# Retention and two feed-forward layers: heads loaded whole, VectorE and GpSimd work of retention in a written order, weight conversions spaced anew

## The chip, the cores and the metric

The kernel runs on one core of a Trainium2 chip. Time is device microseconds (us) from start to end of one execution. Engine names below: TensorE (PE, matrix products; PEld, its loads of weights), VectorE (DVE), ScalarE (ACT), GpSimd (POOL), SyncE (SP, which issues the DMA transfers).

## The reference

Four batches of eight heads, 576 positions of 64 dimensions, go through retention; its output, 2304 rows of 512, goes through two feed-forward layers. Cut to what matters:

```python
scores = (1 / sqrt(64)) * q @ k.T                     # each head, 576 x 576
Dmat   = where(i >= j, gamma[head] ** (i - j), 0)     # decay with distance
ret    = (scores * Dmat) @ v                          # 4 x 8 x 576 x 64
x      = ret.transpose(0, 2, 1, 3).reshape(2304, 512)
h      = ((x @ w1) * (x @ w2)) @ w3                   # 2304 x 1024
x      = h @ w_out                                    # 2304 x 512
h      = x @ w_in                                     # 2304 x 2048
g      = maximum(h, 0) + alpha * minimum(h, 0)
out    = g @ w_out2                                   # 2304 x 512
```

Inputs and output are float32 in the reference; the weights arrive as 64-bit values and are turned into pairs of a rounded high part and a low part on the chip.

## The kernel before

**Stages.** Retention runs from 0 to 126 us. The stage from 126 to 308 us makes (x @ w1) * (x @ w2) in 24 groups (3 parts of x by 8 units of weights), each by seven block products where the plain way takes eight. From 308 to 352 us w3 @ w_out is folded into one matrix, while x still waits; 352 to 452 us multiplies by it. From 452 to 642 us comes x @ w_in with the activation ("stage G" below, groups GGroup), and then g @ w_out2 to the end.

**Retention.** Heads go in pairs, two heads on the two halves of 64 partitions; a batch has four pairs. The sequence is cut into five chunks (four of 128 and one of 64). For one chunk TensorE makes the scores of its positions among themselves (`scores`, L391), VectorE multiplies them by a mask (L395, or L383 for the short chunk); TensorE makes the moments k v of the chunk (`moments`, L406), VectorE adds them to the state aged so far (L412 for the first chunk, L414), GpSimd ages the new state by the decay of a chunk (L418); TensorE makes the values (`values`, L433 from the state, L442 from the masked scores), and ScalarE copies them into x (`parts`, L454). Ahead of that GpSimd scales q by position (`scale`, L368 for 512 columns, L370 for 64), and ScalarE scales k (`prep`, L361). Batch 0 is done in two parts of two pairs (`r0`, `r1`, six steps each); batches 1 to 3 are a chain of fifteen links of four pairs: link i makes the scores of chunk i + 1, the values of chunk i and the moments of chunk i + 1. The PSUM tile of the moments is one, that of the scores is double. The table `beside` says what else stands behind which link: scales of the next batch (`ready`), loads, conversions of the first weights, and operands made of x (`x_steps`).

**Halves.** In x, the two heads of an odd pair stand in the other order than in memory. Before, odd pairs (and their constants) are loaded with their two halves exchanged: `in_places` splits a load into two of 64 rows.

**Buffers of heads.** Batches 0 and 2 share one room (heads_r), 1 and 3 another (heads_l, the last pair elsewhere). So batch 2 loads once batch 0 has been read, and batch 3 once batch 1 has.

**Weights.** A piece of 128 x 512 weights is loaded (raw) and goes through four steps: ScalarE `_first` (L92, L93), VectorE `_second` (L102 to L107, four passes), ScalarE `_third` (the high part), VectorE `_fourth` (the low part, L121). Units of w1 and w2 (`AbUnits`) are two pieces, with VectorE sums of their quarters (`sums`, L564 to L567) and low halves of these (L557). Operands of x are differences (L630), rounded by ScalarE (L622), with low halves on VectorE (L626). Eight pairs of pieces of w_out2 (`ops2`) are converted where there is room: three in the stage from 126 us, five in stage G; each has a multiplication by the sign of alpha (L294), differences (L277) and high and low halves (L245, L254); in the earlier stage VectorE does differences and signs together (L275), in stage G GpSimd does. In stage G the raw pieces (`rawo`) and the results on their way to memory share three buffers.

**Order.** TensorE, ScalarE and SyncE run in the order in which the code is written. VectorE and GpSimd are ordered by a scheduler, by its own estimate of when operands are ready; each engine then runs its row in order. `spot` and `at` place work between products: a group has three positions, a, b and c, and "5b" is position b of group 5. In stage G ScalarE also copies a product bank for the next group's sums (L1260), which TensorE (L779) waits for.

## Time and profile before

| | us |
|---|---|
| median of three runs | 827.45 (825.82 to 829.76) |
| the profiled execution | 826.97 |
| its span on the core | 825.2 |
| TensorE busy | 760.3 (92%) |
| VectorE busy | 627.7 (76%) |
| ScalarE busy | 423.5 (51%) |
| GpSimd busy | 66.8 (8%) |

The stages above are cuts of the span by the first and last products of each. The mean granted clock of TensorE over the span is 0.959 of full speed. In a timeline, the bracket behind an instruction tells how long its engine stood idle ahead of it, and what ended that; SPq is SyncE's issue of a transfer, not the transfer.

### The profile page before, as it was taken

How to read it: one execution, taken by the hardware profiler on the slowest of the kernel's cores; microseconds unless marked ns; L12 is line 12 of the kernel's file. 1: busy time of each engine (PE TensorE's matmuls, PEld its weight loads, DVE VectorE, ACT ScalarE, POOL GpSimd, SP SyncE). 2: the span in 40 equal slices, each digit the busy share in tenths (PEclk: the TensorE clock that was granted, in tenths of full speed). 3: DMA queues.
4: the chain of work that ended last, by engine and by line, in shares of the span. 5: the costliest groups of instructions: out<-in, count | busy, mean ns of one | idle time of the engine just before them, and what ended most of it. 6: DMA issues, size and time to landing. Idle time of an engine off the chain costs nothing.

```text
span 825.2 us, 13389 instructions
## 1 busy us (share of the span) xinstructions
PE 760.3 (92%) x4977; PEld 707.5 (86%) x4979; DVE 627.7 (76%) x1028; ACT 423.5 (51%) x750; POOL 66.8 (8%) x81
## 2 busy tenths in 40 slices
PE   6657579999999999999999969989999999999998
PEld 3546469999999998899999969989999888888887
DVE  1115897899989896998998756877877688887784
ACT  1214446566656654676765635645654454444443
POOL 1422510000000000000000302122020000000000
PEclk8759898999999999999999988999999999999999
DMA  6973801467755798659673888767599954444440
GB/s 159 301 218 105 260 27 36 158 202 243 255 194 175 264 341 320 203 182 401 207 282 120 266 303 282 254 237 250 158 316 378 316 163 127 129 127 128 134 147 26
DMA packets 103249, 173.26 MB, mean 210 GB/s; under 512 B 9872, under 2 KB 68496, under 8 KB 103184
## 3 DMA queue, kind: packets, MB, share of 16 engines
q1 hardware_dynamic: 103184, 172.41, 62.7%
q8 instruction: 39, 0.64, 0.3%
q14 instruction: 26, 0.21, 0.1%
HBM read 112.34 MB, written 60.03 MB: 209 GB/s over the span
## 4 chain that ended last, share of the span: by engine, by line
PE 75%; DMA 12%; DVE 5%; issue 2%; SPq 2%; ACT 2%; POOL 1%; ACTq 0%; DVEq 0%; POOLq 0%
PE h L779 35%; PE o L1369 13%; PE y L1187 12%; PE o L1371 7%; PE pw L1027 5%; DMA heads_r<-in_qk_dram 2%; DMA heads_l<-in_qk_dram 2%; DMA heads_r<-in_kv_dram 2%; DMA cells<-gd 2%; DMA xs<-in_qk_dram 1%; DMA gd<-g 1%; PE o L442 1%; DMA wod<-wo2u 1%; DMA pair<-in_qk_dram 1%; SPq L475 1%
## 5 line engine op out<-in xcount | busy, mean ns | idle before, releaser
L1187 PE MATMUL y<-yab,wa 128*128 128x384 f32 x576 | 100.0, 334 | 0.0
L1187 PEld LDWEIGHTS y<-yab,wa 128*128 128x128 f32 x576 | 99.9, 188 | 0.1
L1350 DVE TENSOR_TENSOR cells<-cells,cells 128x1024 fp32r<-128x1024 f32 x63 | 76.3, 1220 | 26.4 <-ACT cells L1344 26.3
L1369 PE MATMUL o<-wa,cells 128*128 128x512 f32 x288 | 76.6, 393 | 0.0
L1344 ACT CAST cells<-cells 128x1024 fp32r<-128x1024 f32 x63 | 64.9, 1052 | 7.5 <-DVE cells L1337 4.5
L779 PE MATMUL h<-xT,wa 128*128 128x384 f32 x288 | 57.7, 342 | 10.5 <-ACT h L1260 10.5
L779 PEld LDWEIGHTS h<-xT,wa 128*128 128x128 f32 x288 | 51.6, 192 | 11.8 <-ACT h L1260 11.4
L1369 PEld LDWEIGHTS o<-wa,cells 128*128 128x128 f32 x288 | 51.4, 189 | 8.5
L1369 PE MATMUL o<-wop,cells 128*128 128x512 f32 x216 | 57.0, 392 | 0.8 <-DVE cells L1381 0.8
L779 PE MATMUL h<-xB,wa 128*128 128x384 f32 x288 | 57.5, 338 | 0.0
L779 PE MATMUL h<-xl,wa 128*128 128x384 f32 x288 | 54.9, 336 | 1.2 <-ACT h L802 1.2
L779 PE MATMUL h<-wa 128*128 128x384 f32 x264 | 51.1, 342 | 1.3 <-ACT h L802 1.3
L779 PEld LDWEIGHTS h<-xl,wa 128*128 128x128 f32 x288 | 50.1, 188 | 2.4 <-ACT h L802 2.1
L779 PEld LDWEIGHTS h<-xB,wa 128*128 128x128 f32 x288 | 51.4, 191 | 0.0
L779 PEld LDWEIGHTS h<-wa 128*128 128x128 f32 x264 | 47.6, 193 | 1.9 <-ACT h L802 1.9
L294 POOL TENSOR_TENSOR a<-a,al 128x512 f32<-128x512 f32 x10 | 11.0, 1100 | 462.8 <-DVE a L107 462.8
L1369 PEld LDWEIGHTS o<-wop,cells 128*128 128x128 f32 x216 | 39.4, 188 | 8.7 <-issue 1.0
L779 PE MATMUL h<-xr,wa 128*128 128x384 f32 x240 | 45.6, 335 | 1.4 <-DVE xs L818 1.4
L454 ACT COPY xs<-o 128x256 f32<-128x256 f32 (+2 forms) x27 | 11.8, 444 | 68.0 <-PE o L442 62.4
L1371 PEld LDWEIGHTS o<-wa,cells 128*128 128x128 f32 x288 | 41.8, 190 | 3.5
L1371 PE MATMUL o<-wa,cells 128*128 128x256 f32 x288 | 44.5, 282 | 0.0
L1242 DVE SCALAR_TENSOR_TENSOR g<-h,al,g 128x384 f32<-128x384 f32 x48 | 29.4, 612 | 18.9 <-ACT g L1241 17.6
(233 smaller groups left out, 1621.6 us busy)
## 6 DMA issues: line engine op xcount, KB each, us to landing
gd<-g SPq DMA_DIRECT2D x96, 192.0 KB, 4.3
cells<-gd SPq DMA_DIRECT2D x36, 512.0 KB, 5.9
abd<-xs SPq DMA_DIRECT2D x24, 384.0 KB, 2.8
yf<-abd SPq DMA_DIRECT2D x24, 384.0 KB, 6.1
rawi<-in_w_in_dram SPq DMA_DIRECT2D x16, 512.0 KB, 5.9
raw<-in_w_dram SPq DMA_DIRECT2D x14, 512.0 KB, 4.3
wod<-wo2u SPq DMA_DIRECT2D x28, 256.0 KB, 4.5
wa<-wod SPq DMA_DIRECT2D x12, 512.0 KB, 5.7
```

The source lines that it names most:

```text
L294: nc.gpsimd.tensor_tensor(out=a, in0=a, in1=sg[:, i:i + 1].to_broadcast([P, 512]), op=ALU.mult)
L442: nc.tensor.matmul(o[pp, p % 2, m // 2, 0:w], vj, rj, start=(c == 0 and m < 2), stop=True, skip_group_check=True)
L454: nc.scalar.copy(dst, o[:, :, :, lo:up].rearrange("p r i w -> p i r w"))
L475: nc.sync.dma_start(out=t[rows], in_=src[pp])
L779: nc.tensor.matmul(ps, a[:, x, ks], b[:, y, k], start=(fresh and n == 0), stop=(n == 5), skip_group_check=True)
L1027: nc.tensor.matmul(acc[i], a[:, ic], bb, start=(k == 0 and n == 0), stop=(k == C1 - 1 and n == 2))
L1187: nc.tensor.matmul(ys[o], wpc[c][a][:, oc], yab[u][:, bb, c % 2], start=(c == 0 and i == 0), stop=(c == C1 - 1 and i == 2))
L1242: nc.vector.scalar_tensor_tensor(out=g, in0=ps, scalar=sal[:, c], in1=g, op0=ALU.mult, op1=ALU.max)
L1344: nc.scalar.copy(h.bitcast(F32R), self.q[name])
L1350: nc.vector.tensor_tensor(out=l.bitcast(F32R), in0=q[name], in1=h, op=ALU.subtract)
L1369: nc.tensor.matmul(ps, h[:, k], w[k], start=(fresh and k == 0), stop=(k == C1 - 1), skip_group_check=True)
L1371: nc.tensor.matmul(ps[:, 256:], l[:, k], w[k][:, 0:256], start=False, stop=(k == C1 - 1), skip_group_check=True)
```

## The change

Heads and constants are loaded whole: `in_places` goes, every pair takes a q, k load and a k, v load of 128 rows, constants of two pairs come in one load. `places` now gives the rows as loaded, and the other half for an odd pair's output, so values are written to the exchanged half. Pieces of w1 and w2 have the row halves of their odd blocks exchanged to match (`Turned`): three loads each. In retention VectorE and GpSimd run in the written order too (`ordered`). Ages of batch 0 go to VectorE, the others stay on GpSimd; scales of four of the sixteen pairs go to VectorE. The first two units of weights are converted earlier. GpSimd takes: the differences of x, the sums of all units but the first, the low parts of 24 pieces of w3 and w_out (`Pieces._fourth`), and all sums and signs of ops2, four pairs of which (three before) are made ahead of stage G. The steps of these conversions are spaced anew (WS, OPS0, OPS1, `spots`), and in stage G each pair of ops2 takes ten steps instead of seven, with the loads of the next one last. Some VectorE additions from PSUM get a higher priority with the scheduler (`soon`). Pieces of the fold lie at other places (`pieces_at`) and are fetched a little earlier.

The diff, cut to its core:

```diff
@@ -342,8 +335,7 @@
     def places(p):
-        x = p % 2
-        return [(HEADS[(j + x) % 2], HEADS[j], (j + x) % 2) for j in range(2)]
+        return [(HEADS[j], HEADS[(j + p) % 2], j) for j in range(2)]
@@ -353,21 +345,22 @@
+            self.age = nc.gpsimd if b else nc.vector
@@ -493,22 +472,17 @@
-        if p % 2:
-            in_places(p, x, qk[b, p])
-            nc.sync.dma_start(out=y[:, 0:16], in_=kv[b, p, :, 0:16])
-            in_places(p, y[:, 16], kv[b, p, :, 16])
-        else:
-            nc.sync.dma_start(out=x, in_=qk[b, p])
-            nc.sync.dma_start(out=y, in_=kv[b, p])
+        nc.sync.dma_start(out=x, in_=qk[b, p])
+        nc.sync.dma_start(out=y, in_=kv[b, p])
@@ -524,19 +498,30 @@
+    class Turned(Weights):
+        def load_until(self, n):
+            while self.loaded < min(n, len(self.pieces)):
+                i = self.loaded
+                t = self.raw[i] = self.raw_room(i)
+                dst, src = (x.rearrange("p (k n) -> p k n", k=KT) for x in (t, self.pieces[i][0]))
+                nc.sync.dma_start(out=dst[:, 0::2], in_=src[:, 0::2])
+                for a, b in (HEADS, HEADS[::-1]):
+                    nc.sync.dma_start(out=dst[a, 1::2], in_=src[b, 1::2])
+                self.loaded += 1
@@ -558,13 +543,14 @@
         def sums(self, c):
...
+            engine = nc.vector if c == 0 else nc.gpsimd
@@ -648,7 +634,7 @@
-        return x_operands(p, place, in_sums)
+        return x_operands(p, place, in_sums, nc.gpsimd)
@@ -660,28 +646,36 @@
-    nc.sync.dma_start(out=kd, in_=c_row[:, 0:H])
-    load_constants(0)
-    load_constants(1)
+    nc.sync.dma_start(out=al_row, in_=c_row)
+    load_constants(0, 1)
     load_pair(0, 0)
     load_pair(0, 1)
-    load_ages()
-    load_constants(2)
-    load_constants(3)
+    load_constants(2, 3)
...
+    ordered = ExitStack()
+    ordered.enter_context(tc.manual_schedule(engines={mybir.EngineType.DVE, mybir.EngineType.Pool}))
@@ -733,19 +722,22 @@
     beside = {
-        3: [lambda: make.extend(ab_operands(0)), x_steps(1), ready(rs[2], 0, 1, 2, 3), ab_steps(0, "s0")],
...
+        3: [ready(rs[2], 2), ready(rs[2], 3, nc.vector), x_steps(1)],
...
-        8: [ready(rs[3], 0, 1, 2, 3), ab_steps(0, "l0")],
...
+        8: [ready(rs[3], 1), ready(rs[3], 2), ready(rs[3], 3, nc.vector), ab_steps(1, "l0")],
@@ -840,34 +836,44 @@
-    PRE, PAIRS_IN_X = 10, 3
+    PRE, PAIRS_IN_X = 10, 4
...
+        def _fourth(self, i):
+            hi, lo = self.dest.pop(i)
+            nc.gpsimd.tensor_tensor(out=lo, in0=self.ab.pop(i)[0], in1=_f32(hi), op=ALU.subtract)
@@ -1423,11 +1433,13 @@
-        ops2.add(m, 7 * (m - PAIRS_IN_X), ("fx", "sx gx fy", "sy gy h1", "l1 t1 h2", "l2 t3 h3", "l3 h4 x", "l4 y"), m + 1 < C1)
+        ops2.add(m, 10 * (m - PAIRS_IN_X), ("fx", "sx gx fy", "sy gy", "h1 t1", "l1 h2 t3", "l2 h3", "l3 h4", "l4", "x", "y"),
+                 m + 1 < C1)
@@ -1448,12 +1460,9 @@
-    for at_spot in (4, 13, 27, 35):
...
+    spots = ("2a 2b 2c 3a 3b 3c 4a 4b 5a 5b", "8c 9a 9b 9c 10a 10b 10c 11a 11b 11c",
+             "12c 13a 13b 13c 14a 14b 14c 15a 15b 15c", "17c 18a 18c 19a 19c 20a 20b 20c")
```

What the order of the engines' rows becomes, in three places. In these rows a name is that of the room in which an operand lies (heads_r and heads_l are the rooms of the heads, al the constants), and a line is that of its own kernel.

SyncE where batch 1's first pairs are loaded, before (qk is q and k, kv is k and v):

```order
L510 DMA heads_l_98<-in_qk_dram 128x1152
L511 DMA heads_l_98<-in_kv_dram 128x1088
L475 DMA heads_l_98<-in_qk_dram 64x1152 x2
L507 DMA heads_l_98<-in_kv_dram 128x1024
L475 DMA heads_l_98<-in_kv_dram 64x64 x2
```

and after, with the first piece of w1 and w2 (raw0):

```order
L485 DMA heads_r_102<-in_kv_dram 128x1088
L484 DMA heads_l_98<-in_qk_dram 128x1152
L485 DMA heads_l_98<-in_kv_dram 128x1088
L509 DMA raw0_129<-in_w12_dram 128x2x128
L511 DMA raw0_129<-in_w12_dram 64x2x128 x2
```

The odd pair's five transfers are two like the even pair's, and a weight piece has three.

GpSimd around the first links of the chain, before (L368 and L370 are scales, L418 ages; the 128 wide ones are of batch 0):

```order
L370 TENSOR_TENSOR heads_l_98<-heads_l_98 128x64
L418 TENSOR_TENSOR heads_l_98<-heads_l_98,al_72 128x128
L368 TENSOR_TENSOR xs_94<-xs_94,heads_l_98 128x512
L370 TENSOR_TENSOR xs_94<-xs_94,heads_l_98 128x64
L418 TENSOR_TENSOR heads_l_98<-heads_l_98,al_72 128x128
L368 TENSOR_TENSOR heads_r_102<-heads_r_102,heads_l_98 128x512
```

and after (L361 and L363 are scales, L411 ages; the last scale here is of batch 2):

```order
L361 TENSOR_TENSOR xs_94<-xs_94,heads_l_98 128x512
L363 TENSOR_TENSOR xs_94<-xs_94,heads_l_98 128x64
L411 TENSOR_TENSOR heads_l_98<-heads_l_98,al_72 128x256 x2
L361 TENSOR_TENSOR heads_r_102<-heads_r_102,heads_l_98 128x512
L363 TENSOR_TENSOR heads_r_102<-heads_r_102,heads_l_98 128x64
```

No age of batch 0 stands in the row any more, and batch 1's ages come behind all its scales.

ScalarE in stage G, before (h are product banks, a and b the first step of a piece, rawo the raw piece, wo2u the results):

```order
L245 CAST wo2u4_3_4640<-t3_3_4614 128x2x256
L1255 ACTIVATE u23_4660<-h3_1_4620,al_72 128x384
L1241 ACTIVATE g3_4668<-h3_0_4619,al_72 128x384
L1241 ACTIVATE g2_4683<-h2_1_4528,al_72 128x384
L1260 COPY h4_1_4702<-h4_0_4701 128x384
L1255 ACTIVATE p54_4717<-h4_2_4703,al_72 128x384
L1255 ACTIVATE u24_4735<-h4_1_4702,al_72 128x384
L1241 ACTIVATE g4_4743<-h4_0_4701,al_72 128x384
L92 ACTIVATE a8_4747<-rawo8_4642 128x512
L93 ACTIVATE b8_4748<-rawo8_4642 128x512
L1241 ACTIVATE g3_4757<-h3_1_4620,al_72 128x384
L92 ACTIVATE a9_4780<-rawo9_4675 128x512
```

and after (L251 is the old L245, L94 the old L92):

```order
L1265 ACTIVATE p52_4563<-h2_2_4549,al_72 128x384
L94 ACTIVATE a8_4565<-rawo8_4423 128x512
L95 ACTIVATE b8_4566<-rawo8_4423 128x512
L1265 ACTIVATE u22_4585<-h2_1_4548,al_72 128x384
L1249 ACTIVATE g2_4593<-h2_0_4547,al_72 128x384
L94 ACTIVATE a9_4602<-rawo9_4425 128x512
L95 ACTIVATE b9_4603<-rawo9_4425 128x512
L1249 ACTIVATE g1_4612<-h1_1_4476,al_72 128x384
L1270 COPY h3_1_4636<-h3_0_4635 128x384
```

Piece 8 stood in group 4, behind the results of pair 3; it now stands in group 2, and pair 3 is no longer made in this stage.

## Rows read from the trace of the kernel before

**Rows 1.** Stretches of the program, busy us by engine, clock and DMA.

```profile
core 0: us, PE busy (x) PEld busy (x) DVE busy (x) ACT busy (x) POOL busy (x), PEclk, DMA share, GB/s
0.00:126.00 126.00, 82.37 (x1182) 63.52 (x1185) 62.25 (x98) 41.43 (x85) 37.31 (x51) 0.78 0.61 178
20.00:50.00 30.00, 20.34 (x245) 15.49 (x245) 6.26 (x14) 6.19 (x16) 10.74 (x16) 0.67 1.02 299
126.00:308.00 182.00, 178.04 (x1009) 175.75 (x1008) 158.88 (x319) 112.28 (x221) 0.00 (x0) 0.99 0.61 207
452.00:642.00 190.00, 177.01 (x997) 174.49 (x996) 140.04 (x231) 98.76 (x183) 29.53 (x30) 0.97 0.80 271
```

**Rows 2.** PE's waits in retention, 0 to 126 us: total, times, longest.

```profile
PE st L406 <- DVE heads_l L414: 14.6, 4, 4.8
```

**Rows 3.** Timeline, 53 to 58 us: start, us, instruction, idle before and releaser.

```profile
54.83 1.26 POOL L368 TENSOR_TENSOR heads_r<-heads_r,heads_l 128x512 f32<-128x512 f32 x1 [2.81 <-DMA heads_r<-in_qk_dram]
56.32 0.40 POOL L418 TENSOR_TENSOR heads_l<-heads_l,al 128x128 f32<-128x128 f32 x1
56.76 0.29 DVE L414 TENSOR_TENSOR heads_l<-heads_l,st 128x128 f32<-128x128 f32 x1 [8.29 <-POOL heads_l L418]
57.19 0.49 PE L433 MATMUL o<-heads_r,heads_l 64*64 64x64 f32 x8 [6.47 <-DVE heads_l L414]
57.73 0.33 SPq L510 DMA_DIRECT2D heads_r<-in_qk_dram  x1
```

**Rows 4.** Loads by tile: count, KB each, median us from issue to landing.

```profile
heads_r<-in_qk_dram SPq DMA_DIRECT2D x4, 576.0 KB, 4.3
heads_r<-in_kv_dram SPq DMA_DIRECT2D x4, 544.0 KB, 6.2
```

**Rows 5.** Timeline of the start: first load of heads, first full scores.

```profile
5.15 0.58 SPq L510 DMA_DIRECT2D heads_r<-in_qk_dram  x1
16.59 0.80 PE L391 MATMUL sc<-heads_r 64*128 64x128 f32 x4 [5.00 <-POOL heads_r L368]
```

**Rows 6.** Timeline, TensorE in the last batch: first scores of two links.

```profile
107.68 0.94 PE L391 MATMUL sc<-heads_l 64*128 64x128 f32 x12
113.59 0.94 PE L391 MATMUL sc<-heads_l 64*128 64x128 f32 x12
```

**Rows 7.** Instructions by line: busy us, mean ns of one, idle before.

```profile
L626 DVE TENSOR_TENSOR xr<-xs,xr 128x768 fp32r<-128x768 f32 x6 | 5.7, 951 | 4.9 <-ACT xr L622 4.9
L121 DVE TENSOR_TENSOR xs<-xs 128x512 fp32r<-128x512 f32 x10 | 6.8, 681 | 0.0
L565 DVE TENSOR_TENSOR xs<-xs,a 128x256 f32<-128x256 f32 x6 | 2.5, 414 | 0.0
L102 DVE TENSOR_SCALAR a<-a 128x512 f32<-128x512 f32 x15 | 6.2, 417 | 0.0
L294 POOL TENSOR_TENSOR a<-a,al 128x512 f32<-128x512 f32 x10 | 11.0, 1100 | 462.8 <-DVE a L107 462.8
L277 POOL TENSOR_TENSOR t<-a,t 128x256 f32<-128x256 f32 x10 | 8.4, 844 | 0.4
```

**Rows 8.** Timeline, GpSimd and VectorE at once, in two places.

```profile
90.34 1.35 POOL L368 TENSOR_TENSOR heads_l<-heads_l 128x512 f32<-128x512 f32 x1 [2.51 <-DMA heads_l<-in_qk_dram]
90.48 1.49 DVE L102 TENSOR_SCALAR a<-a 128x512 f32<-128x512 f32 x1
69.53 1.22 DVE L395 TENSOR_TENSOR heads_l<-sc,heads_l 128x1024 f32<-128x1024 f32 x1
69.69 0.61 POOL L418 TENSOR_TENSOR heads_l<-heads_l,al 128x256 f32<-128x256 f32 x1 [0.54 <-DVE heads_l L414]
```

**Rows 9.** Timeline of stage G, where TensorE stands longest.

```profile
490.10 0.66 ACT L92 ACTIVATE a<-rawo 128x512 f32<-128x512 f32 x1 [6.31 <-DMA rawo<-in_w_out_dram]
496.25 2.29 PE L779 MATMUL h<-xT,wa 128*128 128x384 f32 x6 [7.88 <-ACT h L1260]
```

**Rows 10.** TensorE's waits in stage G, 452 to 642 us.

```profile
PE h L779 <- ACT h L1260: 12.4, 5, 7.9
```

More of the change, by code (lines that the diff above doesn't have):

```diff
@@ L355, in __init__, with prep @@
             self.rt, self.state = {}, {}
-        def prep(self, pairs=None):
-            for p in pairs or self.pairs:
+            self.age = nc.gpsimd if b else nc.vector
+        def prep(self, pairs):
+            for p in pairs:
                 k = kvt[self.b][p]
@@ L470, in retention_moe_kernel, with load_constants @@
     qt, kt, kvt, vt = ({b: {} for b in range(B)} for _ in range(4))
-    def in_places(p, t, src):
-        for rows, pp, _ in places(p):
-            nc.sync.dma_start(out=t[rows], in_=src[pp])
-    def load_constants(p):
-        if p % 2 == 0:
-            nc.sync.dma_start(out=per_pair[:, p], in_=c_pair[:, p])
-            return
-        in_places(p, qs[:, p], c_pair[:, p, 2 * CH + 64:])
-        for h in range(2):
-            nc.sync.dma_start(out=mask[:, h, p], in_=c_pair[:, p, (1 - h) * CH:(2 - h) * CH])
-        in_places(p, mtail[:, p], c_pair[:, p, 2 * CH:2 * CH + 64])
-    def load_ages():
-        nc.sync.dma_start(out=gc[:, 0::2], in_=c_row[:, H::2])
-        in_places(1, gc[:, 1::2], c_row[:, H + 1::2])
+    def load_constants(*pairs):
+        ps = slice(pairs[0], pairs[-1] + 1)
+        nc.sync.dma_start(out=per_pair[:, ps], in_=c_pair[:, ps])
     def load_pair(b, p):
@@ L680, in retention_moe_kernel, with ready, run @@
     busy(26)
+    rs = [None] + [Retention(b, list(range(NPAIR)), psum0) for b in range(1, B)]
     r0, r1 = Retention(0, [0, 1], psum0), Retention(0, [2, 3], psum0)
     s0, s1 = r0.steps(), r1.steps()
-    r0.scale()
-    r0.prep()
+    def ready(r, p, engine=nc.gpsimd):
+        def run():
+            r.scale([p], engine)
+            r.prep([p])
+        return run
     def keep_busy(step):
@@ L691, in keep_busy @@
         return run
-    def ready(r, *ps):
-        def run():
-            r.scale(ps)
-            r.prep(ps)
-        return run
-    rs = [None] + [Retention(b, list(range(NPAIR)), psum0) for b in range(1, B)]
     chain = [(b, c) for b in range(1, B) for c in range(NCH)]
@@ L712, in link, with ab_steps @@
         return run
+    def ab_steps(c, steps):
+        return lambda: abu.run(c, steps)
     b = keep_busy
-    for step in (b(s0[0]), b(s0[1]), b(s0[2]), b(s0[3]), ready(r1, 2), s0[4], ready(r1, 3), s1[0],
-                 s0[5], s1[1], s1[2], ready(rs[1], 0), s1[3], ready(rs[1], 1), s1[4], ready(rs[1], 2), s1[5],
-                 ready(rs[1], 3)):
+    for p in range(2):
+        ready(r0, p, nc.vector)()
+    for step in (b(s0[0]), b(s0[1]), b(s0[2]), ready(r1, 2), b(s0[3]), ready(r1, 3), s0[4], s1[0], s0[5], s1[1],
+                 ab_steps(0, "f0"), s1[2], ready(rs[1], 0), ab_steps(0, "s0"), s1[3], ready(rs[1], 1), ab_steps(0, "h0 f1"),
+                 s1[4], ready(rs[1], 2), ab_steps(0, "s1 l0"), s1[5], ready(rs[1], 3), ab_steps(0, "h1")):
         step()
@@ L720, in retention_moe_kernel @@
     load_batch(2)
-    abu.load(2)
+    abu.load(4)
     def x_steps(n):
         return lambda: some_of(make, n)
-    def ab_steps(c, steps):
-        return lambda: abu.run(c, steps)
     def to_xr():
@@ L826, in p3 @@
             u = self.f[:, 1]
-            nc.vector.tensor_tensor(out=u, in0=self.b3, in1=u, op=ALU.add)
-            nc.vector.tensor_tensor(out=u, in0=u, in1=self.p5s, op=ALU.mult)
+            with soon():
+                nc.vector.tensor_tensor(out=u, in0=self.b3, in1=u, op=ALU.add)
+                nc.vector.tensor_tensor(out=u, in0=u, in1=self.p5s, op=ALU.mult)
             later.append(self.spill)
@@ L1247, in from_sum @@
             g = self.tile("g", 8)
[L1248 to L1249 removed]
+            with soon():
+                nc.vector.scalar_tensor_tensor(out=g, in0=a, scalar=sg[:, c], in1=b, op0=ALU.mult, op1=ALU.add)
+                nc.vector.scalar_tensor_tensor(out=g, in0=g, scalar=al[:, c], in1=g, op0=ALU.mult, op1=ALU.max)
             keep(2 * self.j + m, 2 * self.p + t, g)
```

204 lines of the change are left out of this document (104 added, 100 removed).

## The prediction

> **What bounds the kernel now.** I read the stretches first, then the waits of TensorE in the stretches where it stands, then the timeline around the longest waits. In the two big product stages TensorE is the bound: from 126 to 308 us it is busy 178.04 of 182.00 us at a clock of 0.99 of full speed, and from 452 to 642 us 177.01 of 190.00 [rows 1]. Retention is another thing. In its 126 us TensorE is busy 82.37, at a clock of 0.78, VectorE 62.25, and the DMA engines 0.61 of the time [rows 1]; nothing is full on the average. From 20 to 50 us the DMA share is 1.02 at 299 GB/s, so there the loads are the bound; later they are not.
>
> The waits say who is late: TensorE's moments L406 wait 14.6 us in four times for VectorE's state addition L414 [rows 2]. The timeline of one more such wait, of the values L433, says why [rows 3]. At 54.83 GpSimd runs a scale L368 after standing 2.81 us for a load; only then does the age L418, queued behind it, run (56.32); VectorE adds at 56.76 after 8.29 idle; TensorE goes on at 57.19 after 6.47; and the next load of a heads' buffer, which needs TensorE's last reads, is issued at 57.73. That is a circle: the load holds GpSimd, GpSimd the state, the state the values, and these the next load. It comes with each batch.
>
> **Retention, part by part.** Removed: the half-row loads and the many constant loads. All pairs now come in two full-height DMAs of 576 and 544 KB, constants in two of 448 KB, and the odd pairs' swap of halves is done where TensorE writes the values, at no instruction. Loads taken as one stream at 299 GB/s [rows 1] plus 2.5 us (taken between nothing and the whole 4.3 or 6.2 us to landing [rows 4], most of which the stream itself hides), and from 1.3 us instead of 5.15 [rows 5], since two issues stand ahead of the first, not eight (5.15 x 2 / 8): pair (0,1) is there after 2.75 MB at 13, where before the first full scores stood at 16.59 after 5.00 us of waiting [rows 5]; batch 1's last pair after 11.1 MB (the other constants and two w12 pieces lie between) at 41; batch 2 after 15.7 MB at 56.
>
> A link (scores, values, moments of one chunk of four pairs) takes (113.59 - 107.68) / 2 = 2.95 us on TensorE where nothing stands [rows 6]. Batch 0's twelve steps have half a link's heads each, so between 1.5 and 2.95; with the middle, 27 us, they end at 39 to 40. So batch 1 starts with its last load at 41.5. Sixteen links would then end at 88.7. They don't quite: batch 3's buffers are those of batch 1, whose last values are read at about 59 (five links from 41.5 give 56.3, and these values stand behind ScalarE's scaling of pair (2,3), which now comes ahead of the copy of o1_3). From 59, 4.59 MB take 15.3 + 2.5 us, so 77; the scale of (3,3), now on VectorE, makes it 78.6, where TensorE would have been ready at 71. Six links of 3.0 to 3.2 follow: 97, the last copies 1.5 more, and the product stage starts at **98.5** for 126 now, the cut of [rows 1]. **Gain 27.5.** The bounds: 91.5 if batch 3's load costs nothing (88.7, 1.3 for the longer last links, 1.5 for the copies), 108.5 if VectorE is the bound (below).
>
> That rests on the ages not being late again. Ages of batch 0 go to VectorE (six of 128x128, at 0.29 each by its addition of that size [rows 3], 1.7 us, in stretches bound by loads); those of the others stay on GpSimd, after all scales of batch 1, and only three scales of each later batch stand among them. A scale of batch 2 can still stand for its load, with an age behind it and TensorE behind that; by the sums above its loads are there at 56 and wanted from 50 to 57, so one wait of up to 3 us is possible and lies inside the 77. VectorE, now in written order, has two such places too, the scales of (2,3) and (3,3), with the tail mask L383 and the next masks L395 behind them and TensorE's values behind these. The w12 pieces take three DMAs of 1 KB rows instead of one each (48 issues for 16); at 0.33 us an issue [rows 3] that is 32 x 0.33 = 10.6 us of SP's time spread over two stages; each is issued a place ahead, so I cost it nothing. If that lead is gone a place costs one landing, 4 to 6 us [rows 4].
>
> VectorE's own work from 41.5 on: 12 masks x 1.22 [rows 8] = 14.6; 13 low halves L626 x 0.951 = 12.4; five low halves of weights and eight conversion passes near 0.681 = 8.9; 15 small ones x 0.413 = 6.2 [rows 7]; two scales near 0.8 each: 44, ending at 85.5. GpSimd's: 9 ages x 0.61 and 6 scales x 1.35 [rows 8] with tails of 0.3; 7 differences of x, 768 wide, at 1.5 x 1.100 and 4 sums x 0.844 [rows 7]: about 31. Side by side both fit under TensorE.
>
> **The stage at 126 to 308.** VectorE loses 24 sums x 0.413, 10 low halves x 0.681 [rows 7] and four differences, and gets a fourth pair of w_out2: 158.88 [rows 1] becomes about 140. GpSimd, at nothing before, gets 40 sums x 0.844, 18 operations x 1.100 [rows 7] and 6 differences x 1.65: 63. TensorE idles only 182.00 - 178.04 = 3.96 there, so no more can come. The earlier place of its additions saves perhaps 2 of these; GpSimd beside VectorE gives them back. **0**, between -3 (a gain) and +21 (below).
>
> What the two do to each other the trace shows in rows: at 90.34 GpSimd's scale and at 90.48 VectorE's pass L102 run together, and L102 takes 1.49 us [rows 8] for 0.417 elsewhere [rows 7]; at 69.53 a mask, whose one source is PSUM, takes its 1.22 beside an age of 0.61, and neither is stretched [rows 8]. [...]
>
> In the fold, 14 low halves go from VectorE to GpSimd: 14 x 0.681 = 9.5 less there, 14 x 1.100 = 15.4 more here [rows 7]; I cost it at nothing, since VectorE is relieved by what GpSimd, idle until then, takes, and at up to 4 if the last piece is late by a few of these. The stages y and out aren't touched.
>
> **Stage 452 to 642.** TensorE idles 190.00 - 177.01 = 12.99 [rows 1], 12.4 of it before L779 for ScalarE's copy L1260, in five waits, the longest 7.9 [rows 10]. The chain: ScalarE stands 6.31 us at 490.10 for a load of rawo, with L1260 behind it, and TensorE begins at 496.25 after 7.88 [rows 9]. Raw pieces and results share three buffers, and the load was asked for one position after the result whose buffer it takes. Now loads stand last of ten steps, three positions after it, and four ahead of their use (a position is 190 / 72 = 2.6 us, so 10.5 against a landing of 4 to 6 [rows 4]); one pair fewer is done here, and the first has its load ahead of the stage. I leave 2.4 of the 12.4 and add 1 for the lower clock after a long stop (0.97 here, 0.99 above [rows 1]): **gain 11**, between 0 and 13.
>
> **Sum.** 825.2 - 27.5 - 0 - 11 = 786.7, and with the 1.8 us that the profiled execution has around its span 788.5: **789**. That execution (826.97) lies 0.5 under the median of the three runs, which changes nothing.
>
> **The rivals.** (a) VectorE becomes the bound of retention: if half of GpSimd's 31 us holds it up, 44 + 15.5 at nine tenths busy is 66 from 41.5, so the stage starts at 108.5: 799. For it: the stretched L102, and a written order that lets nothing pass. Against: masks are free of it, and TensorE waits at the loads anyway. (b) The stop at rawo only moves to another pair: gain 0 there, 800. For it: pair 6 still has its load right behind stores of results on SP. Both: 811. (c) Slower: GpSimd and VectorE take turns throughout. In the stage of 182 us that is 140 + 63 = 203, so 21 more; it decides once what can't overlap adds to more than 182. In retention 44 + 31 at 0.87 from 41.5 gives 128, so 2 more: 827 + 21 + 2 - 11 = 839. For it: L102 at 90.48 [rows 8]. Against: a mask from PSUM lies beside GpSimd untouched [rows 8]; the stage has 72 additions from PSUM of 384 columns, about 0.55 each between 0.413 and 0.681 [rows 7], 39 us, and without these the turns add to 164. (d) Loads come faster than 299 GB/s, batch 3 isn't waited for, the stage starts at 91.5: 782. [...]
>
> **How the numbers follow.** The forecast (780 to 796) has 0.53; (a) 0.17, (b) 0.12, both 0.03, (c) 0.06, (d) 0.09. The range takes all but (c) and the ends: **774 to 813**. It goes below (d) by the 2 us of the second stage and all 13 of the fourth. 0.5% (4 us) is about what a measurement can tell from no change: over that faster 0.91, within 0.03, slower 0.06.
>
> **What would show it.** Right: first AB product at 95 to 102; loads without a gap until batch 1 is in, then one gap until about 59; no age waiting behind a scale for over 3 us; TensorE busy 178 in a stage of 181 to 184; at most 4 us of waits for L1260. Wrong: VectorE busy over nine tenths from 42 to 98 with TensorE waiting for its masks or low halves (a); ScalarE again standing 5 us for rawo (b); the second stage over 190 with L102 and its like at 1 us (c).

## The result and the profile after

The changed kernel takes 809.12 us, median of 4 runs (807.9 to 809.31), beside 827.78 before: a ratio of 0.9771, 95% interval 0.9746 to 0.9797. It is faster, as forecast, and inside the range of 774 to 813, but by 18.7 us where 38.5 were forecast. Half of the gain is missing: the groups of w1 and w2 lost 16.0 of the 38.3 us that retention and stage G won.

Stages of the two profiled executions, from the start of the first product of one stage to that of the next (us):

| stage | before | after | change | forecast |
|---|---|---|---|---|
| retention | 125.5 | 102.2 | -23.3 | -27.5 |
| groups of w1 and w2 | 182.9 | 198.9 | +16.0 | 0 |
| fold | 43.5 | 46.3 | +2.8 | 0 |
| y | 99.9 | 100.1 | +0.2 | 0 |
| stage G | 190.1 | 175.1 | -15.0 | -11 |
| out, to the end of the span | 183.3 | 183.5 | +0.2 | 0 |
| span | 825.2 | 806.1 | -19.1 | -38.5 |

The stretches of the changed kernel in the columns of [rows 1] (length, then busy us of TensorE, its weight loads, VectorE, ScalarE and GpSimd, the clock, the DMA share and GB/s):

```profile
0.00:102.00 102.00, 73.89 (x1174) 58.13 (x1178) 70.16 (x102) 42.18 (x87) 46.88 (x48) 0.88 0.58 214
102.00:301.00 199.00, 182.82 (x1034) 177.93 (x1024) 174.87 (x279) 115.10 (x229) 76.25 (x66) 0.98 0.62 214
...
447.00:622.00 175.00, 173.63 (x997) 172.38 (x996) 133.88 (x218) 96.40 (x176) 24.28 (x24) 1.00 0.81 278
```

In the second row VectorE is busy 174.87 us where the forecast had 140, and GpSimd 76.25 where it had 63; TensorE idles 16 us, against 4 in the same row of [rows 1]. In the third TensorE idles 1.4, against 13.

What TensorE waits for in the second stage, before (total, times, longest):

```profile
PE h L779 <- ACT h L802: 2.6, 2, 1.3
PE h L779 <- DVE xs L818: 1.4, 1, 1.4
```

and after (L812 is the old L818, an addition of VectorE; L795 the old L802, ScalarE's copy of a product bank):

```profile
PE h L772 <- DVE xs L812: 9.5, 8, 3.0
PE h L772 <- ACT h L795: 5.7, 4, 2.3
```

The instructions of VectorE in that stage tell more (line, engine, operation, shapes and count, then busy us, mean ns, idle before):

```profile
L824 DVE TENSOR_TENSOR xs<-xs 128x384 f32<-128x384 f32 x23 | 18.7, 813 | 0.1
...
L817 DVE TENSOR_TENSOR xs<-h,xs 128x384 f32<-128x384 f32 x24 | 13.3, 553 | 11.3 <-PE h L772 11.1
L812 DVE TENSOR_TENSOR xs<-h,xs 128x384 f32<-128x384 f32 x24 | 13.2, 550 | 3.7 <-PE h L772 3.7
...
L612 DVE TENSOR_TENSOR xl<-xs,xl 128x768 fp32r<-128x768 f32 x8 | 11.2, 1406 | 0.7 <-ACT xl L608 0.7
L104 DVE TENSOR_SCALAR xs<-xs 128x512 f32<-128x512 f32 x18 | 10.6, 587 | 2.7 <-ACT xs L94 2.7
```

and of GpSimd in the same stage:

```profile
L271 POOL TENSOR_TENSOR xs<-xs 128x256 f32<-128x256 f32 x16 | 15.6, 998 | 0.5
...
L616 POOL TENSOR_TENSOR xs<-xs 128x768 f32<-128x768 f32 x6 | 12.4, 2067 | 8.9 <-DVE xr L612 5.0 <-DVE xl L612 3.9
```

L824 and L817 have the same 384 columns. L817 takes one source from PSUM (h) and goes at 0.553 us; L824 has both sources in SBUF and takes 0.813. L612 is the old L626, 0.951 in [rows 7], now 1.406; L104 the old L102, 0.417 there, now 0.587. GpSimd's own operations are slow too: a difference of 768 columns was put at 1.65 us and takes 2.067, one of 256 columns takes 0.998 for 0.844 in [rows 7].

In retention the old circle is gone. TensorE's waits up to 130 us (total, times, longest), in the columns of [rows 2]:

```profile
PE o L426 <- ACT xs L447: 12.6, 5, 7.0
PE o L435 <- DVE heads_l L388: 10.4, 5, 3.4
```

No wait for a state addition is left (L407 is the old L414, 14.6 us in [rows 2]). In its place stand waits for ScalarE's copy of the values (L447) and for masks (L388). The two longest, in the timeline (start, us, instruction, idle before and its releaser):

```profile
47.28 0.66 ACT L94 ACTIVATE a<-raw 128x512 f32<-128x512 f32 x1 [8.82 <-DMA raw<-in_w_dram]
48.40 0.58 ACT L447 COPY xs<-o 128x512 f32<-128x512 f32 x1
49.03 0.91 PE L426 MATMUL o<-heads_l 64*64 64x128 f32 x10 [6.98 <-ACT xs L447]
...
76.41 0.18 DVE L833 TENSOR_SCALAR al<-al 128x16 f32<-128x16 f32 x1 [5.78 <-DMA al<-in_alpha_dram]
76.50 1.22 DVE L388 TENSOR_TENSOR heads_l<-sc,heads_l 128x1024 f32<-128x1024 f32 x1
77.77 1.97 PE L435 MATMUL o<-heads_l,heads_r 128*64 128x128 f32 x16 [3.40 <-DVE heads_l L388]
```

ScalarE stands 8.82 us for a weight piece that was asked for behind batch 2's heads, and the copy that TensorE needs is behind it in the row. Later VectorE stands for alpha, asked for behind batch 3's heads, with a mask behind it. Both waits are new, and both are a load's that nobody needs yet. The step on alpha (L833) is written behind the whole of retention, and yet stands in VectorE's row ahead of masks of retention; so it is not the written order that put it there.

### The profile page after: what moved, and what is told of

The parts are those of the page before. It is cut to its first block, busy times and chain, and to the rows that moved or that the text cites. A ratio compares the mean times of both kernels' runs of the same rounds, so it can differ in the third digit from the quotient of the medians.

```text
span 806.1 us, 13426 instructions
## 1 busy us (share of the span) xinstructions
PE 753.7 (93%) x4979; PEld 701.8 (87%) x4979; DVE 649.3 (81%) x966; ACT 422.7 (52%) x750; POOL 164.2 (20%) x149
## 4 chain that ended last, share of the span: by engine, by line
PE 56%; DVE 11%; DMA 4%; issue 3%; ACT 1%; POOL 0%; SPq 0%; DVEq 0%; ACTq 0%; POOLq 0%
PE h L772 23%; PE o L1379 14%; PE y L1195 12%; PE o L1381 7%; DMA cells<-gd 2%; DVE a L107 2%; DVE a L109 1%; DMA abd<-xs 1%; DVE a L104 1%; DMA raww<-in_w3t_dram 1%; DVE xs L107 1%; DVE xs L255 1%; PE pw L1035 1%; DVE a L105 1%; DVE xs L824 1%
## 5 line engine op out<-in xcount | busy, mean ns | idle before, releaser
L772 PE MATMUL h<-xT,wa 128*128 128x384 f32 x288 | 55.8, 335 | 0.8 <-DVE g L1258 0.7
L287 POOL TENSOR_TENSOR a<-a,al 128x512 f32<-128x512 f32 x8 | 8.8, 1099 | 219.3 <-DVE a L109 219.3
L772 PEld LDWEIGHTS h<-xT,wa 128*128 128x128 f32 x288 | 50.3, 188 | 1.4 <-DVE g L1258 1.4
L772 PEld LDWEIGHTS h<-xr,wa 128*128 128x128 f32 x240 | 42.5, 191 | 6.3 <-DVE xs L812 3.9
L109 DVE CUSTOM_DVE_ANT_0 a<-a,b 128x1024 uint16<-128x1024 uint16 x54 | 44.3, 822 | 1.8
```

Source lines behind the costliest of these rows:

```text
L109: nc.vector.tensor_tensor(out=a.bitcast(I32), in0=a.bitcast(I32), in1=b, op=ALU.add)
L287: nc.gpsimd.tensor_tensor(out=a, in0=a, in1=sg[:, i:i + 1].to_broadcast([P, 512]), op=ALU.mult)
L772: nc.tensor.matmul(ps, a[:, x, ks], b[:, y, k], start=(fresh and n == 0), stop=(n == 5), skip_group_check=True)
```

## The experiments

Each was timed in three rounds against the kernel before on the same chip. The texts in quotes were on record before the runs. A result is the median time, its ratio to the kernel before, and in brackets the 95% interval of the ratio. The stage lengths are read as in the table above, one profiled execution each; the recorded texts have some of them 0.2 to 0.4 us off. The six kernels that have the second stage as the change made it (the changed one among them) show 197.3 to 200.5 us in it, the four that have it as before 181.7 to 182.9. So a difference of 2 or 3 us against the first says little, one of 3 against the second more.

**GpSimd alone, in the kernel before.**

```diff
     def do(n, pos):
+        if n > 1:
+            f = pairs_of[(n - 2) % 3]
+            for _ in range(3):
+                nc.gpsimd.tensor_tensor(out=pad, in0=f[:, 0, 0:120], in1=f[:, 1, 0:120], op=ALU.subtract)
```

> The kernel before, with 198 GpSimd subtractions of 120 columns added beside the groups of the second stage; each reads two finished results of an older group in SBUF, nobody waits for their output, and nothing is taken away. Theory 1 (GpSimd holds up VectorE): VectorE's instructions with two SBUF sources stretch (L828, 0.549 us before, to 0.65 and more), those with a PSUM source (L818, L822, L827 at 0.55) don't, VectorE's busy time there rises from 158.9 to 170 to 190, and the stage from 182.7 to 188 to 200: 832 to 845. Rival theory 2 (the stage of the changed kernel grew only by VectorE's own added work and its order): stretched or not, VectorE has room in the stage of the kernel before, which stays under 185: 826 to 830.

848.51 us, ratio 1.0279 (1.0228 to 1.0331): theory 1, past the upper end of what it expected. The stage takes 202.2 us for 182.9. The stretch of that stage, in the columns of [rows 1]:

```profile
124.00:326.00 202.00, 183.70 (x1011) 177.79 (x1012) 187.59 (x321) 112.46 (x223) 133.37 (x198) 0.98 0.56 190
```

and three lines of its instructions:

```profile
L828 DVE TENSOR_TENSOR xs<-xs 128x384 f32<-128x384 f32 x24 | 14.8, 615 | 0.1
...
L822 DVE TENSOR_TENSOR xs<-h,xs 128x384 f32<-128x384 f32 x24 | 13.2, 549 | 5.9 <-POOL pad L962 3.6 <-PE h L779 2.3
...
L962 POOL TENSOR_TENSOR pad<-xs 128x120 f32<-128x120 f32 x198 | 133.4, 674 | 74.2 <-DVE xs L828 60.2
```

VectorE's busy time goes from 158.88 [rows 1] to 187.59 with the same work; L822, with its PSUM source, stays at 0.549. Some of the growth isn't the stretching: L822 waits 3.6 us until GpSimd has read an older result, which the experiment brought in.

**GpSimd's work taken out of the changed kernel's second stage.**

```diff
-            engine = nc.vector if c == 0 else nc.gpsimd
+            engine = nc.gpsimd if c == 1 else nc.vector
-        return x_operands(p, place, in_sums, nc.gpsimd)
+        return x_operands(p, place, in_sums, nc.gpsimd if p < 2 else nc.vector)
```

and in the same way for `_fourth`, the sums and the signs.

> The changed kernel with all that GpSimd does in the stage of the 24 groups put back on VectorE (24 sums of units 2 to 7, the last differences of x, the low parts of the first ten pieces, signs and sums of four w_out2 pairs); order, spacing, priorities and the fourth pair stay, and so do retention, fold and G. Theory 1: the stage grew from 182.7 to 198.7 us because GpSimd holds up VectorE's instructions with two SBUF sources; then VectorE's own work there, about 173 us, goes through at its undisturbed durations (the low half L612 of 768 columns at 0.95 us for 1.41 to 1.75 now, L824 at 0.55 for 0.81), the stage takes 184 to 190 and the time is 796 to 802. Rival: the stage grew because of the new order, the priorities and the fourth pair; then more work on VectorE makes it longer still: over 200 in the stage and over 811.

806.48 us, 0.9737 (0.9709 to 0.9766); the stage 196.6. Both theories miss. Nearly all instructions are back at their undisturbed durations (L824 0.551), and yet only 2.3 us come back, no more than such stages differ by. The stretch of the stage:

```profile
102.00:298.70 196.70, 183.96 (x1025) 181.00 (x1017) 171.48 (x339) 115.36 (x228) 5.41 (x4) 0.97 0.62 213
```

TensorE's waits in it:

```profile
PE h L772 <- ACT h L795: 9.5, 6, 3.5
PE h L772 <- DVE xs L812: 2.0, 1, 2.0
```

and ScalarE's:

```profile
ACT xs L251 <- DVE xs L287: 11.4, 5, 4.2
ACT xs L115 <- DVE xs L109: 11.4, 5, 4.8
```

TensorE, which in the changed kernel waited 9.5 us for VectorE's L812, now waits as long for a bank copy of ScalarE (L795), and ScalarE, in its written order, for passes of VectorE ahead of the high parts L115 and L251. VectorE is busy nearly as long as when it was held, 171.48 us. So theory 1 was true of the instructions and not enough for the stage.

**Without the priority.**

```diff
     def soon():
-        return tc.high_priority(offset=SOON)
+        return ExitStack()
```

> The changed kernel without the higher priority of the additions from PSUM. If the priority orders VectorE's row badly (rival of theory 1), the second stage falls by 5 us or more and the time to 804 or less. By theory 1 the additions then stand behind more stretched work and the time is the same or longer: 808 to 816.

810.12, 0.979 (0.976 to 0.9819), the stage 198.0: taking the priority away shows no difference.

**Three pairs in the stage**, with GpSimd's work and without. `PAIRS_IN_X = 3`, and in stage G:

```diff
+    spots = ("0c 1a 1b 1c 2a 2b 2c 3a 3b 3c", "4a 4b 4c 5a 5b 5c 6a 6b 6c 7a", "8c 9a 9b 9c 10a 10b 10c 11a 11b 11c",
```

> The changed kernel with three pairs of w_out2 in the second stage instead of four, the fourth made in stage G in ten steps from 0c on; GpSimd's work stays where the change put it. Theory 2 (VectorE is full: 174.7 us of work in 196.6 us with GpSimd's work put back, 158.9 in 182.7 before): a pair is about 10 us of VectorE and ScalarE, so the stage falls from 198.7 to 188 to 193, G grows by 0 to 4: 800 to 806. Theory 1 alone: GpSimd still stands beside VectorE with 50 us or more, and the stage stays over 194: 805 to 810.

816.58, 0.9865 (0.9832 to 0.9898).

> As the run with three pairs, and all that GpSimd does in the second stage is put back on VectorE. Theory 2: VectorE has about 165 us there, and by the same share (0.87 to 0.89) the stage takes 184 to 189, G as in the other run: 796 to 803. If GpSimd's work is a net relief, this is longer than the other run by 3 us or more; if it is a net loss (theory 1), shorter by 3 or more; if its hold takes back just what it relieves, the two are within 3.

814.85, 0.9844 (0.9801 to 0.9887). The stages are 199.9 and 196.1, so the fourth pair is not what made the stage longer: theory 2 falls. In the second of these VectorE has only 164.83 us of work in it. Between the two the stage differs by 3.8 us and the time by 1.7, which is too little to price GpSimd's work in the new order. The fold takes 44.3 and 43.6 us for 46.3. Stage G grows to 185.5 and 185.0, in part because ScalarE stands 8.75 and 8.37 us for rawo near its beginning again.

**The pieces a tick apart**, on the version without GpSimd and on the changed kernel. A tick moves each of the pieces of w3 and w_out that are under way by a step. With it the loads of these pieces come at another place too.

```diff
-            for n, step in ((3, self._fourth), (2, self._third), (0, self._first), (1, self._second)):
+            for n, step in ((3, self._fourth), (2, self._third), (1, self._second), (0, self._first)):
                 i = self.at[n]
-                if i < (upto if n == 0 else self.at[0] if n == 1 else before[n - 1]):
+                if i < (upto if n == 0 else before[n - 1]):
```

> As the run with the second stage's GpSimd work put back on VectorE, and the four passes of a w3 or w_out piece on VectorE come one tick (2.4 positions, about 6 us) after its first step on ScalarE instead of in the same tick, its high part another tick later. Theory 3: with GpSimd out of the way the stage is held by ScalarE, which in its written order stands for L109 and for the 'issue' of the copies L115 (11.4 + 3.0 + 4.9 us), with the bank copies L795 behind it and TensorE 9.5 us behind these. Then most of these waits go, TensorE waits 3 to 5 us for L795, and the stage falls from 196.6 to 187 to 192: 797 to 802. Rival (VectorE is full and late whatever its order): ScalarE stands as long elsewhere, the stage stays at 194 to 198: 803 to 808.

806.44, 0.9737 (0.9694 to 0.9779); the stage 193.8, 2.8 less, and the fold 50.3, 1.7 more. The time is that of the run before it (806.48), on the rival's side; the stage lies a little under the rival's 194 to 198. The waits for L109 went, but ScalarE stands 11.9 us for L287 as before, and 6.4 and 3.5 us for loads.

> The changed kernel with only the passes of the pieces a tick apart; GpSimd keeps its work. Theory 3: the two causes add up in the changed kernel; without ScalarE's waits for L109 the stage falls from 198.7 to 193 to 196, and TensorE's 9.5 us of waits for VectorE's L812, which stands behind stretched work, remain: 803 to 807. If GpSimd's hold is the only cause, no change: 808 to 811.

809.73, 0.9773 (0.9726 to 0.9821); the stage 199.6. The waits for L109 went, but the pieces' loads came later with the tick, and ScalarE stood 6.3 and 1.7 us for those. The forecast of no change holds; but since another step of the same chain was late, this does not show that GpSimd's hold is the only cause.

**The old second stage behind the new retention.** The spacing, the rooms of the pieces, three pairs with their signs inside the high and low parts, and VectorE for all of it, as in the kernel before; five pairs in stage G as above.

```diff
-    PRE, PAIRS_IN_X = 10, 4
+    PRE, PAIRS_IN_X = 10, 3
-        ops2.add(j, 7 * j, ("fx", "sx gx fy x", "sy gy y", "h1 t1", "l1 h2 t3", "l2 h3", "l3 h4", "l4"), j + 1 < PAIRS_IN_X)
+        ops2.add(j, 6 * j, ("fx fy sx gx", "sy gy h1", "h2 l1 t1 x y", "h3 l2 t3", "h4 l3", "l4"), j + 1 < PAIRS_IN_X)
```

> The changed kernel's retention, with the second stage as in the kernel before: its spacing and rooms of pieces, three pairs with signs inside the high and low parts, all on VectorE; the fourth pair goes to stage G as in the run with three pairs. Theory 3 (the new spacing and order in the written rows of ScalarE and SyncE, and GpSimd's hold, are the two causes): the stage takes 182 to 185 and the fold 43 to 45, G 185: start 102 + 183.5 + 44 + 99.9 + 185 + 183.5 = 798, so 797 to 803. Rival (what retention leaves behind lengthens the stage): 190 to 196 in the stage: 805 to 812.

797.08, 0.9643 (0.9601 to 0.9684): theory 3. The stage takes 181.8 us, the fold 43.5, G 186.2. Nothing that retention leaves behind lengthens the stage. The 14 low halves of the fold are back on VectorE here too. The stretch of the stage:

```profile
101.10:282.90 181.80, 177.28 (x1020) 175.10 (x1013) 160.44 (x318) 112.43 (x220) 2.49 (x1) 1.00 0.63 211
```

Beside the run with three pairs and next to no GpSimd work (164.83 us of VectorE in 196.1) this has nearly the same work, 160.44, in 14.3 us less. What is left between the two is the spacing and order of the conversions, the separate signs and the rooms of the pieces; the runs don't divide these 14 us further.

**The same with the 24 sums on GpSimd.**

```diff
-            engine = nc.gpsimd if c == 1 else nc.vector
+            engine = nc.vector if c == 0 else nc.gpsimd
```

> As the run with the old second stage, but the 24 sums of units 2 to 7 stay on GpSimd as the change has it. VectorE is relieved of 24 x 0.413 = 9.9 us. Theory 1: GpSimd takes 24 x about 0.9 = 22 us, during which VectorE's passes with two SBUF sources stand, so VectorE's busy time in the stage does not fall (within 4 us of the other run), and the stage is 0 to 5 us longer. Rival: a few operations apart from each other are a net relief; VectorE's busy time falls by 8 to 10 and the stage by 0 to 2.

801.02, 0.9696 (0.9645 to 0.9747): theory 1. The stage is 185.2, 3.4 longer; GpSimd works 27.79 us there for 2.49, and VectorE's busy time falls to 158.68, by 1.8 where 24 x 0.413 = 9.9 were taken from it.

```profile
100.90:286.10 185.20, 178.84 (x1015) 176.54 (x1012) 158.68 (x294) 112.27 (x220) 27.79 (x25) 0.99 0.62 207
```

**Retention: the ages alone, in the kernel before.** L418 on VectorE for all batches.

```diff
-                    nc.gpsimd.tensor_tensor(out=self.aged, in0=new, in1=gc[:, self.ps].unsqueeze(2)
+                    nc.vector.tensor_tensor(out=self.aged, in0=new, in1=gc[:, self.ps].unsqueeze(2)
```

> The kernel before with the ages of all batches on VectorE, and nothing else of the change. If the ages queued behind scales that wait for loads are the main cause of retention's 125.5 us, TensorE's 14.6 us of waits for L414 fall under 4 and the groups start at 108 to 116: 808 to 818. Rival: the loads (half-row transfers, 299 GB/s and the gaps between) set the time, and something else of a batch is late next: the start stays at 121 to 126: 822 to 828.

812.11, 0.9818 (0.9768 to 0.9868): the ages were the main cause. The groups start at 110.1 for 125.5.

```profile
PE o L442 <- DVE heads_l L395: 12.9, 6, 3.5
PE sc L391 <- POOL heads_r L368: 9.0, 3, 5.2
PE st L406 <- DVE heads_l L414: 0.8, 1, 0.8
```

The wait for L414 falls from 14.6 [rows 2] to 0.8; next late are scales that wait for loads.

**Half-row loads in the changed kernel.**

```diff
+        if p % 2:
+            for rows in HEADS:
+                nc.sync.dma_start(out=x[rows], in_=qk[b, p, rows])
+            nc.sync.dma_start(out=y[:, 0:16], in_=kv[b, p, :, 0:16])
+            for rows in HEADS:
+                nc.sync.dma_start(out=y[rows, 16], in_=kv[b, p, rows, 16])
+            return
```

> The changed kernel with the odd pairs' heads loaded in two halves of 64 rows again (without an exchange; the pair (3,3) and the constants stay whole). If whole loads carry the earlier start, the loads run at about 300 GB/s from 10 to 40 us where the changed kernel has 359 to 413, batch 1's first scores come at 37 to 41 for 33.5, and the groups start 3 to 7 us later: 811 to 816. Rival: the number of issues and the ages were all: within 2 us of 102 and 807 to 811.

817.77, 0.9883 (0.9841 to 0.9925), start of the groups 110.6, 8.4 later than in the changed kernel. That is the first theory, a little past its upper ends (7 us and 816). The DMA engines are as busy, and carry less. The changed kernel from 20 to 40 us:

```profile
20.00:30.00 10.00, 6.85 (x132) 5.50 (x128) 8.80 (x16) 4.74 (x11) 4.66 (x6) 1.00 1.04 359
30.00:40.00 10.00, 6.28 (x79) 5.44 (x77) 7.71 (x13) 4.90 (x11) 1.99 (x3) 0.66 1.02 405
```

and with half-row loads:

```profile
20.00:30.00 10.00, 8.67 (x168) 7.04 (x169) 6.72 (x16) 4.85 (x12) 2.34 (x3) 1.00 1.04 316
30.00:40.00 10.00, 2.53 (x40) 1.93 (x38) 4.24 (x8) 4.07 (x9) 3.54 (x5) 0.68 1.02 292
```

From 10 to 20 us it is 365 for 413. Batch 1's first scores come at 39.1 for 33.5, 5.6 us later. The rest of the 8.4 goes with a wait that the changed kernel has already: ScalarE stands 14.22 us for 8.82 for the weight piece behind batch 2's heads, and TensorE 12.37 for 6.98 behind it. An odd pair's heads take five transfers here for two, so half rows and a larger number of transfers are not told apart.

**The two new waits of retention.** The third piece of w1 and w2 loaded ahead of batch 2:

```diff
+    abu.load(3)
     load_batch(2)
```

> The changed kernel with the third piece of w1 and w2 loaded ahead of batch 2 instead of behind it. In the trace ScalarE stands 8.82 us for that piece (47.28), the copy of o1_0 behind it and TensorE 6.98 behind that. If this new wait in the written order is what retention lacks of the forecast, the wait falls under 1 us, batch 1 ends 6 to 7 us sooner, batch 3's loads are asked for at about 54 instead of 60.57, and the stage starts at 96 to 98: 803 to 805. Rival: batch 3 and VectorE's later waits take it all; then the start stays at 101 to 103 and the time at 808 to 810.

803.14, 0.9699 (0.9674 to 0.9724), groups from 95.2: the wait was on the path. Alpha loaded at the start:

```diff
     load_constants(2, 3)
+    nc.sync.dma_start(out=al, in_=alpha)
...
-    nc.sync.dma_start(out=al, in_=alpha)
```

> The changed kernel with alpha loaded at the start. In the trace VectorE's row, now in written order, stands 5.78 us for alpha (76.41) with a mask behind it and TensorE 3.40 behind that. If that wait is on the path, the stage of the groups starts 3 to 5 us sooner, at 97 to 99: 804 to 806. Rival: batch 3's heads, whose scales run at 79.72 to 85, set the end anyway; then 808 to 810.

803.52, 0.9698 (0.967 to 0.9726), groups from 97.3: on the path too. Both together (the two edits above):

> The changed kernel with both the third piece of w1 and w2 ahead of batch 2 and alpha at the start. If the two waits stand one after the other on the path (6.7 and 5 us sooner alone), the groups start at 90 to 92 for 102.2 and the time falls by the sum as far as the second stage doesn't give it back: 796 to 800. Rival: both were cover for the same load of batch 3; then 95 to 97 and 801 to 804.

799.36, 0.9666 (0.9635 to 0.9696), groups from 90.4. The waits stood one after the other: 7.0 and 4.9 us alone, 11.8 together. The span gains 9.1 of these (806.1 to 797.0): the second stage is 1.6 shorter, but the fold 3.3 and G 1.4 longer. With both gone, VectorE is nearly full from 42 us on:

```profile
42.00:90.00 48.00, 36.31 (x729) 31.32 (x729) 45.04 (x48) 23.24 (x46) 36.73 (x31) 0.96 0.37 134
```

**Stage G in the old steps.**

```diff
-        ops2.add(m, 10 * (m - PAIRS_IN_X), ("fx", "sx gx fy", "sy gy", "h1 t1", "l1 h2 t3", "l2 h3", "l3 h4", "l4", "x", "y"),
+        ops2.add(m, 7 * (m - PAIRS_IN_X), ("fx", "sx gx fy", "sy gy h1", "l1 t1 h2", "l2 t3 h3", "l3 h4 x", "l4 y"), m + 1 < C1)
```

The positions of the steps go with it: `spots` has four of the five rows of seven that the kernel before had.

> The changed kernel with stage G's four pairs in the old seven steps, the next pair's loads one position behind the results whose buffers they take. If the place of the loads made stage G shorter (175.5 us for 190.3), ScalarE stands 4 to 6 us again for rawo, TensorE behind L1270 by 5 to 9 us in all, and G takes 181 to 187: 815 to 822. Rival: one pair fewer did it; then G stays under 178: 808 to 811.

818.37, 0.9879 (0.9838 to 0.9921): the place of the loads. G takes 185.1 us, and the old picture of [rows 9] is back, with four pairs:

```profile
491.00 0.66 ACT L94 ACTIVATE a<-rawo 128x512 f32<-128x512 f32 x1 [4.52 <-DMA rawo<-in_w_out_dram]
492.64 2.29 PE L772 MATMUL h<-xT,wa 128*128 128x384 f32 x6 [7.27 <-ACT h L1270]
```

**What they point to**: both loads early, the old second stage, five pairs in G in ten steps with gaps between them. Beside the edits above:

```diff
+    spots = ("0c 1a 1b 1c 2a 2b 2c 3a 3b 3c", "4c 5a 5b 5c 6a 6b 6c 7a 7b 7c", "9a 9b 9c 10a 10b 10c 11a 11b 11c 12a",
+             "13a 13b 13c 14a 14b 14c 15a 15b 15c 16a", "17c 18a 18c 19a 19c 20a 20b 20c")
```

> The version that the runs point to: the changed kernel's retention with the third piece of w1 and w2 and alpha loaded early, the second stage as before with no work on GpSimd, and five pairs in stage G in ten steps with gaps, so that each raw piece is asked for at least four positions ahead. By sums: start 90.5, stage 183 to 186, fold 44, next 99.9, G 177 to 180, the last 183.5 and 1.8 around: 780 to 787. If the second stage depends on when retention ends, or G stands for rawo again, 790 to 797.

780.45, 0.9436 (0.939 to 0.9482): faster than both kernels, by 48 and 29 us. Its stretches of retention, groups and G (180.0 us, with five pairs; ScalarE still stands 4.61 us for a load of rawo early in it):

```profile
0.00:91.00 91.00, 71.46 (x1172) 56.48 (x1178) 72.10 (x102) 42.38 (x87) 48.97 (x48) 0.92 0.66 240
91.00:273.00 182.00, 177.48 (x1036) 175.24 (x1027) 160.90 (x318) 112.81 (x220) 2.72 (x2) 1.00 0.64 211
416.00:596.00 180.00, 175.71 (x998) 174.11 (x997) 141.21 (x230) 99.89 (x184) 29.71 (x30) 0.99 0.81 286
```

## Why the prediction was right and wrong

**The second stage: wrong, and the step that failed.** The term "0, between -3 and +21" was +16.0: TensorE's waits there grew by 12.2 us, and its products took 3.8 us longer (busy 182.72 for 178.94, at 0.98 for 0.99 of the full clock). The 0 took VectorE's own work, 140 us of 182, as leaving room, and it had no term for the new order and spacing of the conversions: of these the prediction has only that "the earlier place of its additions saves perhaps 2", and nothing of what ScalarE waits for.

The new order is the larger part that the runs show. With three pairs and GpSimd's work taken out, the stage takes 196.1 us in the new order and 181.8 in the old, 14.3 more for nearly equal work; there TensorE waits for ScalarE, and ScalarE for VectorE's passes and signs. Which part of the new order it is (the spacing, the separate signs, the rooms of the pieces) stays open; a tick more between the passes gave 2.8 us in the stage and nothing in the time.

GpSimd's hold is real, and its worth depends on the order. The 140 was right as work: with all of it on VectorE the stage has 171.48, and what GpSimd does in the changed kernel is 32.6 of that (24 sums 10.0, 16 differences and 8 signs 11.9, 10 low halves 6.9, four differences of x 3.8), which leaves 139. The other 36 of the 174.87 are hold, which the forecast left out of its term. In the old order 24 sums on GpSimd lengthen the stage by 3.4 us, and TensorE's waits for ScalarE's bank copy and VectorE's additions grow from 4.5 to 6.3. In the new order, where the stage is 16.0 longer, taking nearly all of GpSimd's work out gives 2.3 back. So the two causes do not add. What GpSimd's whole share would cost in the old order was not run.

Rival (c) named the hold, and its +21 came near the +16.0 by luck: it knew nothing of the order, and taking its cause away gives back little. Its condition, that what can't overlap adds to more than 182, was put too high as well: 25 us of GpSimd's sums beside 159 of VectorE's, some 39 of which take a source from PSUM, add to about 145, and already lengthen the stage.

Both sides of rival (c) show in the runs: additions of 384 columns with a PSUM source stayed at 0.55 us beside GpSimd and without it (0.549 to 0.553 in the changed kernel, 0.551 to 0.555 with GpSimd's work taken out), the ones with two SBUF sources went from 0.551 to 0.813 beside the changed kernel's GpSimd. What no sentence of the forecast drew from this is that the sums moved to GpSimd return only a part of what they took: 1.8 of 9.9 us.

**Retention: right in sign and cause; the size is near by two errors that cancel.** The ages behind scales were the circle: moved alone they give 15.4 us. The loads were put at 299 GB/s and batch 1 at 41.5; they ran at 359 to 413 from 10 to 40 us, and batch 1's first scores stood at 33.52. Rival (d) had the faster loads right, but not its start at 91.5; half rows again cost 8.4 us, in part through the wait for a weight piece. What a transfer of 64 rows costs by itself can't be read from this, since only about a quarter of the heads' bytes goes in halves. What the faster loads gained was lost to two waits that the forecast did not have: one for a weight piece among those it named as "issued a place ahead", one for alpha. With these gone the groups start at 90.4, under the lower bound of 91.5. The wait of up to 3 us for a scale of batch 2 did not come up.

**Stage G: right in its mechanism, small in one term.** The gain is 15.0 for 11, past the upper bound of 13. TensorE's idle time fell by 11.6, and its products, 997 in both, are busy 173.63 us for 177.01, with the clock at 1.00 for 0.97: the term for the clock, put at 1, was 3.4. In the kernel before the clock reads 0.50 from 496.3 to 500 us, right behind the stop of [rows 9], 0.89 from there to 505 and 1.00 to 512. The term for the waits left 2.4 us and found 1.3, for a VectorE step. The place of the loads is worth 10.0 (185.1 in the old steps with four pairs), the fifth pair 5.0 (190.1 to 185.1). Rival (b) was wrong here, and came true in the runs with five pairs, where the load stands early in the stage.

**The fold:** 0, up to 4, was 2.8. The low halves on GpSimd alone are not the reason: with three pairs in the stage ahead they are still there, and the fold takes 44.3 and 43.6. It goes with the fourth pair; why was not tried apart. **Rival (a)** did not come in the changed kernel: VectorE is busy 39.40 of the 56 us from 42 to 98, and its longest hold of TensorE in retention was a wait for a load. With both waits gone it is near: VectorE is busy 45.04 of 48 us, and TensorE waits 8.9 us for masks.

Three small sums of the prediction are off, without weight for the argument: 41.5 and 66 make 107.5 and not the 108.5 of rival (a), (a) and (b) together make 810 and not 811, and 782 less 2 us for each of the two product stages makes 778, not the 774 of the range.

## What to carry to other kernels

Sums moved from VectorE to GpSimd were not off VectorE for nothing here: taking 9.9 us away gave 1.8 back and made the stage 3.4 us longer. What GpSimd holds up belongs into the sum. The new order of work had a price too, though no engine was full: a step that waited for a load (8.82 and 5.78 us) or for a pass just issued (up to 4.8, with GpSimd's work taken out) held what stood behind it in its engine's row, here the copy or the mask that TensorE needs. Asking for such a load earlier gave 4.9 and 7.0 us. And test a change of several parts one at a time: ages, whole loads and the place of the loads in G each paid, and the new order of the second stage cost, which the sum hid.

## What was not expected of the hardware

Full-height loads of half a MB one behind the other, with some weight pieces between, ran at 359 to 413 GB/s from 10 to 40 us; with the odd pairs' q, k loads in halves of 64 rows it was 365, 316 and 292, with the same share of busy DMA engines (1.02 to 1.04). And GpSimd and VectorE slowed each other: in the kernel before, an age of 256 columns on GpSimd took 0.61 us beside a mask [rows 8] and 1.26 at 72.36 beside a VectorE subtraction with both sources in SBUF (L630, 0.95 from 72.20 on), and with the 198 subtractions added on GpSimd VectorE's L828 went from 0.549 to 0.615. In the changed kernel's second stage a GpSimd subtraction of 768 columns took 2.067, 1.81 at the shortest and 2.49 at the longest, and VectorE's L824 0.813 for 0.551; the L824 beside the subtraction of 117.61 took 2.19.
